# The 64 tokens left over by chunks of 1024: loads of their own, or a ninth token in half of the last chunk's partitions

## The chip, the cores and the metric

The kernel runs on one core of a Trainium2 chip. The metric is the time of one execution on the device, in microseconds (us), as the median of three runs. The profile is that of one further execution; its times count from its first instruction.

## What is computed

Four batches of 6208 tokens with 256 channels go through an attention over channels and then a mixture of depths, in which only 128 tokens of each batch pass a small network:

```python
qn = q / (np.linalg.norm(q, axis=1, keepdims=True) + 1e-06)      # norms over the tokens
kn = k / (np.linalg.norm(k, axis=1, keepdims=True) + 1e-06)
s = kn.transpose(0, 2, 1) @ qn / tau                             # 256 x 256 for each batch
a = softmax(s)                                                   # over the last axis
x = v @ a                                                        # tokens x 256
scores = x @ w_gate
top_idx = np.argpartition(-scores[b], 128)[:128]                 # the 128 best of each batch
ye = np.maximum(x[b, top_idx] @ w1, 0.0) @ w2
out = x;  out[b, top_idx] += sigmoid(scores[b, top_idx])[:, None] * ye
```

q, k, v and the output are fp32 in HBM, 25.4 MB each. The kernel computes in bf16 with fp32 sums.

## The kernel before, in words

**Tiles.** The tokens of a batch are cut into 6 full chunks of 1024 (`CHUNK`, `NFULL` = 6) and 64 tokens that are left over (`REM`). A full chunk is a tile of 128 partitions with 8 tokens in each (`RPP` = 8): partition p holds tokens 8p to 8p + 7 of the chunk, which lie one behind the other in HBM, so that a load is one run of 8 KB for each partition. The leftover tokens are a seventh chunk (`ci == NFULL`) with a tile of its own (`q_rem`, `k_rem`, `v_rem`, `stage_rem` from `rem_pool`), one token in each of 64 partitions.

**Loads.** `emit_load` issues them from GpSimd's queue[...]: 512 KB as written for a full chunk, 32 KB for a leftover. `units` lists them in the order of use, and `pump` issues the next one while buffers are free (4 for q and k, 6 for v, 2 for the leftovers of each kind) and no more than 11 tiles are ahead (`AHEAD`). When the last step that reads a chunk has been written, `consumed` gives its buffer back. The very last chunk of q and k (`halved`) is loaded in two halves of its tokens. Each load also waits until the load eight issues earlier has landed, as eight semaphores go round.

**First pass** (`p1_steps`): for each token row of a chunk, six matmuls add k'q, q'q and k'k to two PSUM tiles (L303, L305, L307). After a batch's last row, which is the leftover's, the softmax follows in stages (`softmax_stages`), put between the matmuls of the next batch.

**Second pass**: `p2_transpose` turns four token rows of v by TensorE and copies them from PSUM (`vt_sb`, L414 to L420), `p2_score` gives the gate's score for each token (L439), `p2_out` the output rows (L485), which ScalarE copies into a store tile (`stage`, L493). A store of a chunk is 1 MB from SyncE's queue (`emit_store`, L559). Batches 0 and 1 do this while the next batch is in its first pass; batch 2 does part of it, and batch 3 all of it, in the tail.

**Selection** (`select_stages`): a search over thresholds on VectorE finds the 128 best tokens, and a one-hot matmul gathers for each its place: `mps` holds for each chosen token a column's number of tokens before it and its partition. The token's row number `idx` is put together from the column (`toff`, by the weights `wrow`), the partition times 8, or the partition alone where the token is a leftover one (`fl`, L653 to L656). By this number the rows of v are gathered (L660), pass the network (`mlp_stages`), and are scattered over the stored output (L729), once the stores of that batch have landed.

**What stands late.** Batch 1 (`H`) keeps its chunks 4 and 5 in SBUF; its chosen tokens are added there by a one-hot matmul (`late_onehot`, `late_mm`), and these two chunks are stored last of all, chunk 5 in two halves. Chunk 3 of batch 1 and the first chunks of batch 2 are held back until the last loads are nearly through (`flush_deferred`): the stores are made to wait for the fourth and third last entry of `units`, chunks 3 and 4 of v of batch 3. In the tail SyncE's queue thus holds, in this order: chunk 3 of batch 1 in quarters, six chunks of batch 2, two leftovers, six chunks of batch 3, chunk 4 of batch 1, chunk 5 of batch 1 in halves.

All instructions stand in the order in which the program writes them (`plan`); no scheduler moves them.

Of the kernel before, what the change touches and what calls it, by code (L numbers as in the profile page):

```python
# [9 lines left out]
F32 = mybir.dt.float32  # L10
BF16 = mybir.dt.bfloat16
# [3 lines left out]
ALU = mybir.AluOpType  # L15
AX = mybir.AxisListType

P = 128
RPP = 8
CHUNK = RPP * P  # L20
# [6 lines left out]
def kernel(  # L27
# [28 lines left out]
    QK_BUFS = 4  # L56
    V_BUFS = 6
    ST_BUFS = 8
    VT_BUFS = 22
    EARLY = 4  # L60
    HOLD = 3
    AHEAD = 11
# [23 lines left out]
    v_flat = v.rearrange("b n c -> (b n) c")  # L86
    out_flat = out.rearrange("b n c -> (b n) c")

    def view(t, b, ci):
        if ci < NFULL:  # L90
            return t[b, ci * CHUNK:(ci + 1) * CHUNK, :].rearrange("(p s) c -> p s c", s=RPP)
        return t[b, NFULL * CHUNK:N, :]

# [54 lines left out]
    plan += [("tail",)] + T[:2] + rest[:1] + T[2:4] + [("adv",), ("a", L)] + T[4:6] + rest[1:2]  # L148
    plan += T[6:8] + W + T[8:10] + S[:6] + T[10:] + rest[2:3] + [("side",)] + S[6:]
    rest = rest[3:]  # L150
    units = []
    for op in plan:
        if op[0] in ("p1", "T"):
            u = ("qk", op[1], op[2]) if op[0] == "p1" else ("v", op[1], op[2][0])
            if u not in units:
                units.append(u)
    loaded = {}
    load_inst = {}
    state = {"next": 0, "qk": 0, "v": 0, "qkr": 0, "vr": 0}
    ahead = [0]  # L160
    limit = {"qk": QK_BUFS, "v": V_BUFS, "qkr": 2, "vr": 2}

    def bucket(kind, ci):
        return kind if ci < NFULL else kind + "r"

    halved = ("qk", B - 1, NFULL - 1)

    def emit_load(u):
        kind, b, ci = u
        tiles = []  # L170
        for nm, src in ((("q", q), ("k", k)) if kind == "qk" else (("v", v),)):
            if ci < NFULL:
                pool = qk_pool if kind == "qk" else v_pool
                t = pool.tile([P, RPP, C], BF16, name=f"{nm}_ch")
                if u != halved:
                    ins = nc.gpsimd.dma_start(out=t, in_=view(src, b, ci))  # L176
            else:
                t = rem_pool.tile([P, 1, C], BF16, name=f"{nm}_rem")
                ins = nc.gpsimd.dma_start(out=t[:REM, 0, :], in_=view(src, b, ci))
            tiles.append(t)  # L180
        if u == halved:
            h = RPP // 2
            for half in (slice(0, h), slice(h, RPP)):
                for t, src in zip(tiles, (q, k)):
                    ins = nc.gpsimd.dma_start(out=t[:, half, :], in_=view(src, b, ci)[:, half, :])
        loaded[u] = tiles
        load_inst[u] = ins

    def pump(most=1000):
        while state["next"] < len(units) and most > 0:  # L190
            u = units[state["next"]]
            bk = bucket(u[0], u[2])
            if state[bk] >= limit[bk] or ahead[0] >= AHEAD:
                return
            emit_load(u)
            ahead[0] += 2 if u[0] == "qk" else 1
            state[bk] += 1
            state["next"] += 1
            most -= 1

    def consumed(u):
        state[bucket(u[0], u[2])] -= 1
        ahead[0] -= 2 if u[0] == "qk" else 1
        pump()

# [51 lines left out]

    wrow = const.tile([P, B, NCOL + 1], F32)
    nc.vector.memset(wrow, 1.0)
    nc.vector.memset(wrow[:, :, RPP - 1:NCOL - 1:RPP], float(CHUNK - RPP + 1))  # L260
    nc.vector.memset(wrow[:, :, NCOL - 1:NCOL], 0.0)
    for b in range(B):
        nc.vector.memset(wrow[:, b, NCOL:NCOL + 1], float(b * N))
# [3 lines left out]
    for i in range(NSTEP):  # L267
# [11 lines left out]
    nc.vector.tensor_copy(rhs[:, NCOL + 2:NCOL + 3], iota_col)  # L279
    ones_col = const.tile([P, NCOL], BF16)  # L280
    nc.vector.memset(ones_col, 1.0)

# [5 lines left out]
    def p1_steps(b, ci):  # L288

        if b not in acc:  # L290
            acc[b] = (ps_s.tile([P, 2, C], F32, name="s_ps"), ps_g.tile([P, 4, P], F32, name="g_ps"))
        s_ps, g_ps = acc[b]
        qt, kt = loaded[("qk", b, ci)]
        rows = RPP if ci < NFULL else 1
        parts = P if ci < NFULL else REM

        def step(s):
            first = ci == 0 and s == 0
            last = ci == NFULL
            qs, ks = qt[:parts, s, :], kt[:parts, s, :]  # L300
            for cc in range(2):
                sl = slice(cc * P, (cc + 1) * P)
                nc.tensor.matmul(s_ps[:, cc, :], lhsT=ks[:, sl], rhs=qs,  # L303
                                 start=first and cc == 0, stop=last and cc == 1)
                nc.tensor.matmul(g_ps[:, cc, :], lhsT=qs[:, sl], rhs=qs[:, sl],  # L305
                                 start=first and cc == 0, stop=False)
# [100 lines left out]
    def p2_transpose(b, g, on_act=False):  # L407
        ci, s0, n = g
        parts = P if ci < NFULL else REM
        vt = loaded[("v", b, ci)][0]  # L410
        vt_ps = vt_psum()
        for j in range(n):
            for cc in range(2):
                nc.tensor.transpose(vt_ps[:, cc, j, :parts], in_=vt[:parts, s0 + j, cc * P:(cc + 1) * P],  # L414
                                    identity=ident_b[:parts, :parts])
# [115 lines left out]

    def late_onehot(idx):

        base = float(H * N + LATE[0] * CHUNK)
        at = moe.tile([P, 1], F32, name="late_at")
        nc.vector.tensor_copy(at, idx)
        nc.vector.tensor_scalar(out=at, in0=at, scalar1=-base, scalar2=1.0 / RPP, op0=ALU.add, op1=ALU.mult)
        onehot = moe.tile([P, len(LATE), RPP, P], BF16, name="late_onehot")
        for i in range(len(LATE)):
            at_row = moe.tile([P, RPP], F32, name=f"late_at_row{i}")  # L540
            nc.vector.tensor_scalar(out=at_row, in0=iota_row[:, 0:RPP], scalar1=-1.0 / RPP, scalar2=at,
                                    op0=ALU.mult, op1=ALU.add)
            nc.vector.tensor_tensor(out=onehot[:, i, :, :], in0=iota_row[:, None, :].to_broadcast([P, RPP, P]),
                                    in1=at_row[:, :, None].to_broadcast([P, RPP, P]), op=ALU.is_equal)
            if i + 1 < len(LATE):
                nc.vector.tensor_scalar(out=at, in0=at, scalar1=-float(P), scalar2=None, op0=ALU.add)
        late_moe.append(onehot)

    def emit_store(b, ci, rows=(0, RPP), count=1):
        st = stage_of[(b, ci)]  # L550
        pieces = []
        if ci == NFULL:
            pieces.append((view(out, b, ci), st[:REM, 0, :]))
        else:
            n = (rows[1] - rows[0]) // count
            for r in range(rows[0], rows[1], n):
                pieces.append((view(out, b, ci)[:, r:r + n, :], st[:, r:r + n, :]))
        for dst, src in pieces:
# [11 lines left out]
    def select_stages(b):  # L570
# [55 lines left out]
        with nc.allow_low_precision(reason="counts of at most 49 are whole in bf16"):  # L626
# [26 lines left out]
        nc.vector.scalar_tensor_tensor(out=fl, in0=toff, scalar=float(b * N + NFULL * CHUNK) - 0.5,  # L653
                                       in1=mps[:, NCOL + 1:NCOL + 2], op0=ALU.is_lt, op1=ALU.mult)
        idx = moe.tile([P, 1], I32, name="idx", bufs=3)
        nc.vector.tensor_scalar(out=idx, in0=mps[:, NCOL + 2:NCOL + 3], scalar1=fl, scalar2=toff,  # L656
                                op0=ALU.max, op1=ALU.add)
# [121 lines left out]
    def flush_deferred():  # L779
# [1 line left out]

        first = len(stores)
        emit_store(*deferred.pop(0), count=4)
        for piece, u in ((first, units[-4]), (first + 2, units[-3])):
            tc.add_manual_dep(
                stores[piece][1].ins, load_inst[u].ins.name,
                mybir.DependencyInfo(mybir.DependencyClass.Sync, mybir.DependencyReason.DATA),
# [6 lines left out]
    def do_p1(b, ci, s):  # L794
        if s == 0:
            pump()
            using(("qk", b, ci))
        steps = p1_steps(b, ci)
        steps[s]()
        spent(0.43)  # L800
        if s == len(steps) - 1:
            consumed(("qk", b, ci))

    def do_transpose(b, g, on_act=False):
        using(("v", b, g[0]))
        vts[(b, g)] = p2_transpose(b, g, on_act)
        if g[1] == 4 or g[0] == NFULL:
            consumed(("v", b, g[0]))
        spent(0.11 * g[2])

    def do_score(b, g):
# [129 lines left out]
```

## Time and profile before

| | |
|---|---|
| time, median of 3 runs | 261.95 us (261.92 to 263.41) |
| span in the profile | 260.1 us |
| TensorE busy with matmuls | 201.7 us, 78% |
| VectorE, ScalarE, GpSimd busy | 49%, 32%, 21% |
| moved by DMA | 66.84 MB, mean 257 GB/s |
| loads with a cast (GpSimd's queue) | 12384 packets, 38.93 MB |
| stores (SyncE's queue) | 4768 packets, 27.53 MB |
| loads of a full chunk of v | 24, 14.8 us from issue to landing in the median |
| loads of a leftover of v | 4, 16.8 us |
| stores of a full chunk | 22, 8.0 us |

The megabytes of a load with a cast are those that it writes, bf16; it reads twice as many. The time from issue to landing of one transfer is mostly its wait in the queue behind others. In the stretches that the prediction shows, DMA's share is the mean busy share of the core's 16 DMA engines; a little over 1 means that the records of neighbouring packets overlap.

### The profile page before, as it was taken

The numbers are of one execution on the slowest core, as the hardware profiler recorded it, in microseconds if no ns is written. First come the engines' busy times: TensorE is split into PE (matmuls) and PEld (weight loads), VectorE is DVE, ScalarE is ACT, GpSimd is POOL, SyncE is SP. The second block draws the span as 40 slices with busy tenths as digits, with TensorE's granted clock in tenths as the row PEclk, the third lists the DMA queues.
The fourth block names the chain that finished last, engine by engine and source line by source line (L and its number), as shares of the span: only waits on it lengthen the run. The fifth ranks groups of instructions, "written<-read, shape, count | busy, mean of one in ns | idle before, by whom it ended". The sixth has DMA issues, their size and how long they took to land.

```text
span 260.1 us, 6113 instructions
## 1 busy us (share of the span) xinstructions
PE 201.7 (78%) x2586; PEld 177.3 (68%) x2586; DVE 126.9 (49%) x474; ACT 84.3 (32%) x149; POOL 55.6 (21%) x104
## 2 busy tenths in 40 slices
PE   0199668889938688698997888799999878889920
PEld 0088557789927476598996677698999668568710
DVE  0300003624403366622436888666685865887830
ACT  3700000167720000107770100434110964878010
POOL 7104124121110023222300325230334003001110
PEclk9999999999976589689999999999999999999995
DMA  7999999999999999999999999999999999999980
GB/s 240 262 213 212 212 212 214 215 214 281 317 317 317 304 213 213 214 212 210 292 316 273 214 212 223 212 213 214 212 210 212 217 257 419 402 412 391 415 369 1
DMA packets 17181, 66.84 MB, mean 257 GB/s; under 512 B 2050, under 2 KB 3587, under 8 KB 14211
## 3 DMA queue, kind: packets, MB, share of 16 engines
q0 software_dynamic: 12384, 38.93, 75.0%
q1 hardware_dynamic: 4768, 27.53, 26.2%
q8 instruction: 20, 0.33, 0.4%
q14 instruction: 7, 0.05, 0.0%
q10 hardware_dynamic: 2, 0.00, 0.0%
HBM read 78.91 MB, written 25.95 MB: 403 GB/s over the span
## 4 chain that ended last, share of the span: by engine, by line
DMA 57%; PE 16%; issue 15%; DVE 6%; POOL 2%; POOLq 1%; ACT 0%
DMA k_ch<-in_k_dram 22%; DMA q_ch<-in_q_dram 18%; DMA v_ch<-in_v_dram 12%; PE s_ps L303 4%; PE o_ps L485 4%; DMA out_dram<-upd,idx 3%; DMA out_dram<-stage 2%; PE g_ps L307 2%; PE g_ps L305 2%; PE vt_ps L414 2%; DVE cnt L610 1%; DVE cmp L606 1%; PE sc_ps L439 1%; DVE junk L322 1%; PE m_ps L354 1%
## 5 line engine op out<-in xcount | busy, mean ns | idle before, releaser
L303 PE MATMUL s_ps<-q_ch,k_ch 128*128 128x256 bf16 x384 | 95.4, 289 | 20.9 <-DMA k_ch<-in_k_dram 20.3
L305 PE MATMUL g_ps<-q_ch 128*128 128x128 bf16 x384 | 88.1, 229 | 1.1 <-DVE nsq L322 1.0
L307 PE MATMUL g_ps<-k_ch 128*128 128x128 bf16 x384 | 88.1, 229 | 0.0
L303 PEld LDWEIGHTS <-k_ch 128*128 128x128 bf16 x384 | 39.7, 103 | 26.8 <-DMA k_ch<-in_k_dram 23.9
L485 PE MATMUL o_ps<-a_sb,vt_sb 128*128 128x256 bf16 (+1 forms) x322 | 47.1, 271 | 2.0 <-ACT vt_sb L418 1.3
L493 ACT COPY stage<-o_ps 128x512 f32<-128x512 f32 x75 | 42.2, 590 | 15.9 <-PE o_ps L485 15.8
L307 PEld LDWEIGHTS <-k_ch 128*128 128x128 bf16 x384 | 39.7, 103 | 8.2 <-issue 1.6
L305 PEld LDWEIGHTS <-q_ch 128*128 128x128 bf16 x384 | 39.6, 103 | 1.2 <-issue 0.9
L420 DVE COPY vt_sb<-vt_ps 128x1024 bf16<-128x1024 bf16 (+1 forms) x35 | 22.2, 637 | 31.5 <-PE vt_ps L414 31.5
L485 PEld LDWEIGHTS <-vt_sb 128*128 128x128 bf16 (+1 forms) x392 | 30.5, 97 | 8.3 <-issue 4.5
L318 ACT COPY s_sb<-s_ps 128x512 f32<-128x512 f32 x4 | 2.3, 585 | 85.3 <-PE s_ps L303 55.1
L439 PEld LDWEIGHTS <-vt_sb 128*128 128x128 bf16 x392 | 25.3, 96 | 2.7 <-DVE sc L574 0.2
L414 PEld LDWEIGHTS <-v_ch 128*128 128x128 bf16 x384 | 22.2, 97 | 5.6 <-DMA v_ch<-in_v_dram 4.4
L439 PE MATMUL sc_ps<-aw_sb,vt_sb 128*128 128x2 bf16 x392 | 25.7, 164 | 0.0
L176 POOL DMA_DIRECT2D q_ch<-in_q_dram x23 | 12.7, 553 | 60.3 <-PE g_ps L307 40.6
L414 PE MATMUL vt_ps<-ident_b,v_ch 128*128 128x128 bf16 x336 | 24.6, 219 | 1.2 <-ACT vt_sb L418 0.7
L322 DVE CUSTOM_DVE_ANT_0 junk<-g_ps,ident_f 128x128 bf16<-128x128 f32 x16 | 4.6, 290 | 34.8 <-PE g_ps L307 34.4
L176 POOL DMA_DIRECT2D v_ch<-in_v_dram x24 | 12.8, 539 | 23.8 <-DMA q_ch<-in_q_dram 11.0
L176 POOL DMA_DIRECT2D k_ch<-in_k_dram x23 | 12.5, 544 | 22.8 <-PE o_ps L485 10.6
L418 ACT COPY vt_sb<-vt_ps 128x1024 bf16<-128x1024 bf16 x11 | 10.6, 1012 | 14.1 <-PE vt_ps L414 14.0
L610 DVE TENSOR_REDUCE cnt<-cmp 128x7 bf16<-128x343 bf16 x28 | 14.4, 513 | 1.0
L606 DVE SCALAR_TENSOR_TENSOR cmp<-u,delta,shares 128x343 bf16<-128x343 f32 x24 | 13.9, 579 | 0.9
(161 smaller groups left out, 214.5 us busy)
## 6 DMA issues: line engine op xcount, KB each, us to landing
out_dram<-stage SPq DMA_DIRECT2D x22, 1024.0 KB, 8.0
v_ch<-in_v_dram POOLq DMA_DIRECT2D x24, 512.0 KB, 14.8
q_ch<-in_q_dram POOLq DMA_DIRECT2D x23, 512.0 KB, 16.8
k_ch<-in_k_dram POOLq DMA_DIRECT2D x23, 512.0 KB, 16.9
stage<-in_moe_w_dram SPq DMA_DIRECT2D x2, 1024.0 KB, 7.0
out_dram<-stage SPq DMA_DIRECT2D x4, 256.0 KB, 5.6
out_dram<-stage SPq DMA_DIRECT2D x2, 512.0 KB, 6.2
q_ch<-in_q_dram POOLq DMA_DIRECT2D x2, 256.0 KB, 9.0
```

What stands on the lines that cost most here:

```text
L176: ins = nc.gpsimd.dma_start(out=t, in_=view(src, b, ci))
L303: nc.tensor.matmul(s_ps[:, cc, :], lhsT=ks[:, sl], rhs=qs, start=first and cc == 0, stop=last and cc == 1)
L305: nc.tensor.matmul(g_ps[:, cc, :], lhsT=qs[:, sl], rhs=qs[:, sl], start=first and cc == 0, stop=False)
L307: nc.tensor.matmul(g_ps[:, 2 + cc, :], lhsT=ks[:, sl], rhs=ks[:, sl], start=False, stop=last and cc == 1)
L414: nc.tensor.transpose(vt_ps[:, cc, j, :parts], in_=vt[:parts, s0 + j, cc * P:(cc + 1) * P], identity=ident_b[:parts, :parts])
L418: nc.scalar.copy(vt_sb[:, :, :n, :parts], vt_ps[:, :, :n, :parts])
L420: nc.vector.tensor_copy(vt_sb[:, :, :n, :parts], vt_ps[:, :, :n, :parts])
L439: nc.tensor.matmul(sc_ps[:parts, col, :], lhsT=vt_sb[:, cc, j, :parts], rhs=aw_sb[:, cc, :], start=cc == 0 and col in (0, NCOL - 1), stop= ...
L485: nc.tensor.matmul(o_ps[:parts, pj, :], lhsT=vt_sb[:, cc, j, :parts], rhs=a_sb[:, cc, :], start=pj == 0 and cc == 0, stop=pj == m - 1 and ...
L493: nc.scalar.copy(st[:parts, s0 + pair * 2:s0 + pair * 2 + m, :], o_ps[:parts, :m, :])
L606: nc.vector.scalar_tensor_tensor(out=cmp, in0=wide, scalar=delta, in1=thr, op0=ALU.subtract, op1=ALU.is_ge)
L610: nc.vector.tensor_reduce(out=cnt, in_=cmp, axis=AX.X, op=ALU.add)
```

## The change

The leftover tokens get no tile and no load of their own. The last full chunk and the 64 tokens behind it are taken as one chunk of 1088 tokens: partitions 0 to 63 hold nine tokens each, partitions 64 to 127 eight. All chunk tiles of q, k and v get room for a ninth row. Since the two halves of the partitions have runs of different length, the chunk is loaded in two transfers (`pieces`), one for partitions 0 to 63 and one for 64 to 127; the halved last chunk of q and k in four transfers each of 64 partitions in place of two of 128. Twelve small loads go, and twelve chunk loads become two each.

The computation keeps its seventh step: the ninth row is read where the leftover tile was read, with 64 partitions. The output's ninth row keeps its tile `stage_rem` and its store of 64 KB, now to 64 rows of HBM that lie nine apart. The store of a last chunk is in two transfers as well; that of batch 1's last chunk, which was in two halves, in four. For the larger tiles the transposed v gets 20 buffers in place of 22. The partition's first token is now 9p for p up to 64, and 8p + 64 beyond; `wrow`, `rhs`, the last steps to `idx` and `late_onehot` follow that.

```diff
-    VT_BUFS = 22
+    VT_BUFS = 20
...
+    def pieces(t, b, ci, rows):
+        if ci < NFULL - 1:
+            v = t[b, ci * CHUNK:(ci + 1) * CHUNK, :].rearrange("(p s) c -> p s c", s=RPP)
+            return [(v[:, rows[0]:rows[1], :], slice(0, P), slice(*rows))]
+        mid = (NFULL - 1) * CHUNK + REM * (RPP + 1)
+        lo = t[b, (NFULL - 1) * CHUNK:mid, :].rearrange("(p s) c -> p s c", s=RPP + 1)
+        got = [(lo[:, rows[0]:rows[1], :], slice(0, REM), slice(*rows))]
+        if rows[0] < RPP:
+            hi = t[b, mid:N, :].rearrange("(p s) c -> p s c", s=RPP)
+            rows = (rows[0], min(rows[1], RPP))
+            got.append((hi[:, rows[0]:rows[1], :], slice(REM, P), slice(*rows)))
+        return got
...
-    limit = {"qk": QK_BUFS, "v": V_BUFS, "qkr": 2, "vr": 2}
+    limit = {"qk": QK_BUFS, "v": V_BUFS}
...
-            if ci < NFULL:
-                pool = qk_pool if kind == "qk" else v_pool
-                t = pool.tile([P, RPP, C], BF16, name=f"{nm}_ch")
-                if u != halved:
-                    ins = nc.gpsimd.dma_start(out=t, in_=view(src, b, ci))
-            else:
-                t = rem_pool.tile([P, 1, C], BF16, name=f"{nm}_rem")
-                ins = nc.gpsimd.dma_start(out=t[:REM, 0, :], in_=view(src, b, ci))
...
+        tiles = [pool.tile([P, RPP + 1, C], BF16, name=f"{nm}_ch") for nm, _ in srcs]
+        top = RPP + (ci == NFULL - 1)
+        for rows in [(0, RPP // 2), (RPP // 2, top)] if u == halved else [(0, top)]:
+            for t, (_, src) in zip(tiles, srcs):
+                for dram, parts, rr in pieces(src, b, ci, rows):
+                    ins = nc.gpsimd.dma_start(out=t[parts, rr, :], in_=dram)
...
-            qs, ks = qt[:parts, s, :], kt[:parts, s, :]
+            row = s if ci < NFULL else RPP
+            qs, ks = qt[:parts, row, :], kt[:parts, row, :]
...
         if ci == NFULL:
-            pieces.append((view(out, b, ci), st[:REM, 0, :]))
+            dram, parts, _ = pieces(out, b, NFULL - 1, (RPP, RPP + 1))[0]
+            todo.append((dram, st[parts, :, :]))
         else:
             n = (rows[1] - rows[0]) // count
             for r in range(rows[0], rows[1], n):
-                pieces.append((view(out, b, ci)[:, r:r + n, :], st[:, r:r + n, :]))
+                for dram, parts, rr in pieces(out, b, ci, (r, r + n)):
+                    todo.append((dram, st[parts, rr, :]))
...
-        for piece, u in ((first, units[-4]), (first + 2, units[-3])):
+        for piece, u in ((first, units[-3]), (first + 2, units[-2])):
...
-        if s == len(steps) - 1:
-            consumed(("qk", b, ci))
+        if s == len(steps) - 1 and ci != NFULL - 1:
+            consumed(("qk", b, home(ci)))
```

In `late_onehot` three small VectorE instructions are added, which work out the first token of each partition; the last two instructions before the gather (`fl`, `idx`) keep their number.

More of the change, by code (lines that the diff above doesn't have):

```diff
@@ L87 @@
     out_flat = out.rearrange("b n c -> (b n) c")
-    def view(t, b, ci):
-        if ci < NFULL:
-            return t[b, ci * CHUNK:(ci + 1) * CHUNK, :].rearrange("(p s) c -> p s c", s=RPP)
-        return t[b, NFULL * CHUNK:N, :]
+    def pieces(t, b, ci, rows):
[10 more added lines that the diff above has]
+        return got
     def groups(ci):
@@ L150, with home @@
     rest = rest[3:]
+    def home(ci):
+        return min(ci, NFULL - 1)
     units = []
@@ L153 @@
         if op[0] in ("p1", "T"):
-            u = ("qk", op[1], op[2]) if op[0] == "p1" else ("v", op[1], op[2][0])
+            u = ("qk", op[1], home(op[2])) if op[0] == "p1" else ("v", op[1], home(op[2][0]))
             if u not in units:
@@ L158 @@
     load_inst = {}
-    state = {"next": 0, "qk": 0, "v": 0, "qkr": 0, "vr": 0}
+    state = {"next": 0, "qk": 0, "v": 0}
     ahead = [0]
-    limit = {"qk": QK_BUFS, "v": V_BUFS, "qkr": 2, "vr": 2}
-    def bucket(kind, ci):
-        return kind if ci < NFULL else kind + "r"
+    limit = {"qk": QK_BUFS, "v": V_BUFS}
     halved = ("qk", B - 1, NFULL - 1)
@@ L169, in emit_load @@
         kind, b, ci = u
-        tiles = []
-        for nm, src in ((("q", q), ("k", k)) if kind == "qk" else (("v", v),)):
-            if ci < NFULL:
-                pool = qk_pool if kind == "qk" else v_pool
-                t = pool.tile([P, RPP, C], BF16, name=f"{nm}_ch")
-                if u != halved:
-                    ins = nc.gpsimd.dma_start(out=t, in_=view(src, b, ci))
-            else:
-                t = rem_pool.tile([P, 1, C], BF16, name=f"{nm}_rem")
-                ins = nc.gpsimd.dma_start(out=t[:REM, 0, :], in_=view(src, b, ci))
[L180 to L185, printed above, removed]
+        srcs = (("q", q), ("k", k)) if kind == "qk" else (("v", v),)
+        pool = qk_pool if kind == "qk" else v_pool
+        tiles = [pool.tile([P, RPP + 1, C], BF16, name=f"{nm}_ch") for nm, _ in srcs]
[4 more added lines that the diff above has]
+                    ins = nc.gpsimd.dma_start(out=t[parts, rr, :], in_=dram)
         loaded[u] = tiles
@@ L191, in pump @@
             u = units[state["next"]]
-            bk = bucket(u[0], u[2])
+            bk = u[0]
             if state[bk] >= limit[bk] or ahead[0] >= AHEAD:
@@ L201, in consumed @@
     def consumed(u):
-        state[bucket(u[0], u[2])] -= 1
+        state[u[0]] -= 1
         ahead[0] -= 2 if u[0] == "qk" else 1
@@ L259 @@
     nc.vector.memset(wrow, 1.0)
-    nc.vector.memset(wrow[:, :, RPP - 1:NCOL - 1:RPP], float(CHUNK - RPP + 1))
+    nc.vector.memset(wrow[:, :, RPP - 1:NCOL - 2:RPP], float(CHUNK - RPP + 1))
     nc.vector.memset(wrow[:, :, NCOL - 1:NCOL], 0.0)
@@ L278 @@
                             scalar2=None, op0=ALU.mult)
-    nc.vector.tensor_copy(rhs[:, NCOL + 2:NCOL + 3], iota_col)
+    nc.vector.tensor_scalar(out=rhs[:, NCOL + 2:NCOL + 3], in0=iota_col, scalar1=float(REM),
+                            scalar2=None, op0=ALU.min)
     ones_col = const.tile([P, NCOL], BF16)
@@ L292, in p1_steps @@
         s_ps, g_ps = acc[b]
-        qt, kt = loaded[("qk", b, ci)]
+        qt, kt = loaded[("qk", b, home(ci))]
         rows = RPP if ci < NFULL else 1
@@ L409, in p2_transpose @@
         parts = P if ci < NFULL else REM
-        vt = loaded[("v", b, ci)][0]
+        vt = loaded[("v", b, home(ci))][0]
+        row = s0 if ci < NFULL else RPP
         vt_ps = vt_psum()
@@ L413, in p2_transpose @@
             for cc in range(2):
-                nc.tensor.transpose(vt_ps[:, cc, j, :parts], in_=vt[:parts, s0 + j, cc * P:(cc + 1) * P],
+                nc.tensor.transpose(vt_ps[:, cc, j, :parts], in_=vt[:parts, row + j, cc * P:(cc + 1) * P],
                                     identity=ident_b[:parts, :parts])
@@ L532, in late_onehot @@
     def late_onehot(idx):
-        base = float(H * N + LATE[0] * CHUNK)
         at = moe.tile([P, 1], F32, name="late_at")
         nc.vector.tensor_copy(at, idx)
-        nc.vector.tensor_scalar(out=at, in0=at, scalar1=-base, scalar2=1.0 / RPP, op0=ALU.add, op1=ALU.mult)
+        first = moe.tile([P, D], F32, name="gy")[:, 0:P]
         onehot = moe.tile([P, len(LATE), RPP, P], BF16, name="late_onehot")
-        for i in range(len(LATE)):
+        for i, ci in enumerate(LATE):
+            if ci < NFULL - 1:
+                nc.vector.tensor_scalar(out=first, in0=iota_row, scalar1=float(RPP), scalar2=None, op0=ALU.mult)
+            else:
+                nc.vector.tensor_scalar(out=first, in0=iota_row, scalar1=float(REM), scalar2=None, op0=ALU.min)
+                nc.vector.scalar_tensor_tensor(out=first, in0=iota_row, scalar=float(RPP), in1=first,
+                                               op0=ALU.mult, op1=ALU.add)
             at_row = moe.tile([P, RPP], F32, name=f"late_at_row{i}")
-            nc.vector.tensor_scalar(out=at_row, in0=iota_row[:, 0:RPP], scalar1=-1.0 / RPP, scalar2=at,
-                                    op0=ALU.mult, op1=ALU.add)
-            nc.vector.tensor_tensor(out=onehot[:, i, :, :], in0=iota_row[:, None, :].to_broadcast([P, RPP, P]),
+            nc.vector.tensor_scalar(out=at_row, in0=iota_row[:, 0:RPP], scalar1=float(H * N + ci * CHUNK),
+                                    scalar2=None, op0=ALU.add)
+            nc.vector.tensor_scalar(out=at_row, in0=at_row, scalar1=-1.0, scalar2=at, op0=ALU.mult, op1=ALU.add)
+            nc.vector.tensor_tensor(out=onehot[:, i, :, :], in0=first[:, None, :].to_broadcast([P, RPP, P]),
                                     in1=at_row[:, :, None].to_broadcast([P, RPP, P]), op=ALU.is_equal)
-            if i + 1 < len(LATE):
-                nc.vector.tensor_scalar(out=at, in0=at, scalar1=-float(P), scalar2=None, op0=ALU.add)
         late_moe.append(onehot)
@@ L550, in emit_store @@
         st = stage_of[(b, ci)]
-        pieces = []
+        todo = []
         if ci == NFULL:
-            pieces.append((view(out, b, ci), st[:REM, 0, :]))
+            dram, parts, _ = pieces(out, b, NFULL - 1, (RPP, RPP + 1))[0]
+            todo.append((dram, st[parts, :, :]))
         else:
@@ L556, in emit_store @@
             for r in range(rows[0], rows[1], n):
-                pieces.append((view(out, b, ci)[:, r:r + n, :], st[:, r:r + n, :]))
-        for dst, src in pieces:
+                for dram, parts, rr in pieces(out, b, ci, (r, r + n)):
+                    todo.append((dram, st[parts, rr, :]))
+        for dst, src in todo:
             ins = nc.sync.dma_start(out=dst, in_=src)
@@ L652, in select_stages @@
         fl = moe.tile([P, 1], F32, name="fl")
-        nc.vector.scalar_tensor_tensor(out=fl, in0=toff, scalar=float(b * N + NFULL * CHUNK) - 0.5,
-                                       in1=mps[:, NCOL + 1:NCOL + 2], op0=ALU.is_lt, op1=ALU.mult)
+        nc.vector.scalar_tensor_tensor(out=fl, in0=toff, scalar=float(b * N + (NFULL - 1) * CHUNK) - 0.5,
+                                       in1=mps[:, NCOL + 2:NCOL + 3], op0=ALU.is_ge, op1=ALU.mult)
         idx = moe.tile([P, 1], I32, name="idx", bufs=3)
-        nc.vector.tensor_scalar(out=idx, in0=mps[:, NCOL + 2:NCOL + 3], scalar1=fl, scalar2=toff,
-                                op0=ALU.max, op1=ALU.add)
+        nc.vector.tensor_scalar(out=idx, in0=mps[:, NCOL + 1:NCOL + 2], scalar1=fl, scalar2=toff,
+                                op0=ALU.add, op1=ALU.add)
         yield
@@ L796, in do_p1 @@
             pump()
-            using(("qk", b, ci))
+            using(("qk", b, home(ci)))
         steps = p1_steps(b, ci)
@@ L800, in do_p1 @@
         spent(0.43)
-        if s == len(steps) - 1:
-            consumed(("qk", b, ci))
+        if s == len(steps) - 1 and ci != NFULL - 1:
+            consumed(("qk", b, home(ci)))
     def do_transpose(b, g, on_act=False):
-        using(("v", b, g[0]))
+        using(("v", b, home(g[0])))
         vts[(b, g)] = p2_transpose(b, g, on_act)
-        if g[1] == 4 or g[0] == NFULL:
-            consumed(("v", b, g[0]))
+        if (g[1] == 4 and g[0] != NFULL - 1) or g[0] == NFULL:
+            consumed(("v", b, home(g[0])))
         spent(0.11 * g[2])
```

## The prediction

> **What bounds the kernel now.** I read the page's slices and its queue table first, then busy time by stage, then the chain of waits near the end, then single transfers with their time from issue to landing. The slices say whether a resource ever rests:
>
> ```profile
> PE   0199668889938688698997888799999878889920
> DMA  7999999999999999999999999999999999999980
> ...
> q0 software_dynamic: 12384, 38.93, 75.0%
> q1 hardware_dynamic: 4768, 27.53, 26.2%
> ...
> DMA 57%; PE 16%; issue 15%; DVE 6%; POOL 2%; POOLq 1%; ACT 0%
> ```
>
> TensorE has holes; the 16 DMA engines have none between the second slice and the 38th. The two queues (q0: loads that cast fp32 to bf16, issued by GpSimd; q1: stores, issued by SyncE) add up to 101% of 16 engines' span, and the chain is mostly DMA. So the time is the engine time of all transfers, some 4 us at the start and some 6 us after the last one. By stage (the columns are stretch, us, busy time of each engine, PEclk, DMA share, GB/s):
>
> ```profile
> 10.00:60.00 50.00, 38.96 (x491) 34.97 (x492) 8.34 (x36) 8.82 (x15) 11.70 (x22) 1.00 1.07 213
> 60.00:90.00 30.00, 22.09 (x269) 19.59 (x267) 9.34 (x25) 10.30 (x19) 3.70 (x7) 0.81 1.04 314
> 141.00:209.00 68.00, 59.04 (x829) 52.86 (x828) 51.79 (x194) 18.59 (x36) 18.11 (x32) 1.00 1.08 214
> 216.00:252.00 36.00, 29.72 (x321) 24.29 (x318) 26.21 (x90) 20.74 (x41) 4.93 (x5) 1.00 1.01 410
> 252.00:260.00 8.00, 0.00 (x0) 0.00 (x0) 0.00 (x0) 0.00 (x0) 0.00 (x0) 0.55 0.11 45
> ```
>
> Loads alone move 213 to 214 GB/s (counted at the bf16 side), loads beside stores 314, stores alone 410. From 216 to 252 us nothing but stores and a few gathers and scatters runs, with the engines full: engine time added there moves the end one for one. The chain agrees (start, us, what):
>
> ```profile
> 188.18 10.43 DMA k_ch<-in_k_dram
> 198.62 0.28 issue
> 198.90 16.20 DMA v_ch<-in_v_dram
> ...
> 230.03 5.89 DMA out_dram<-stage
> ...
> 243.05 6.80 DMA out_dram<-upd,idx
> ```
>
> Loads set it up to 215.1 us, stores and scatters afterwards. The last two transfers are level: the last store is issued at 248.9 and lands 5.2 us later (254.1), the last scatter at 250.6 and lands 3.8 later (254.4).
>
> [...] Does the trace agree? The only 64-partition stores in it are those of the leftover tokens:
>
> ```profile
> out_dram<-stage_rem SPq DMA_DIRECT2D x4, 64.0 KB, 6.2
> q_rem<-in_q_dram POOLq DMA_DIRECT2D x4, 32.0 KB, 19.9
> ```
>
> Two of them run back to back in the full tail. The 1 MB store ahead of them, issued at 225.7, lands after 7.4 us (233.1); the 1 MB store behind, issued at 230.0, after 5.9 (235.9). That is 2.8 us for 1 MB and 128 KB; stores of 1 MB alone land 2.45 us apart. So the 128 KB took about 0.35 us: 0.31 at 410 GB/s[...]. The windows say the same:
>
> ```profile
> 228.00:230.30 2.30, 1.72 (x16) 1.24 (x14) 2.09 (x8) 1.78 (x4) 0.00 (x0) 1.00 1.02 417
> 230.30:233.10 2.80, 2.22 (x21) 1.84 (x21) 2.28 (x11) 2.21 (x5) 0.00 (x0) 1.00 0.98 392
> 233.10:236.00 2.90, 2.82 (x30) 2.30 (x28) 1.70 (x9) 2.90 (x7) 0.08 (x1) 1.00 1.01 424
> ```
>
> The dip from 417 to 392 is small. But these are 8 KB an engine[...], and the engines aren't in step: the packets of the two stores, 46 ns each and 8 to an engine, are spread from 230.4 to 233.0 us. So the trace [...] doesn't show 64 partitions of half a megabyte.
>
> **The change part by part.**
>
> 1. Twelve leftover loads go (q, k and v of four batches, 32 KB each). Three landings price one: k issued at 188.2 lands after 10.4 (198.6), the q leftover issued at 188.7 after 10.1 (198.8), the k leftover at 189.2 after 9.8 (199.0): 0.2 us each. 12 x 0.2 = 2.4 us of load queue, all on the path.
>
> 2. The same bytes come back as a ninth token in 64 partitions: 32 KB at 214 GB/s is 0.15 us, 12 x 0.15 = 1.8 us. Net -0.6 us. If the longer rows (4608 bytes) are cut in two it is 0; if the ninth token rode for nothing, -2.4.
>
> 3. The last chunk's loads are two transfers of 64 partitions. [...] I take no cost. [...]
>
> 4. GpSimd issues 2 DMAs more (the halved last q and k become 8 issues where 4 and 2 leftovers stood). An issue takes 0.53 us and up to eight are in flight, 10 to 16 us ahead of their landing; the issues hide behind the queue. A load waits for the landing of the one eight issues back; with 128 KB pieces in the ring the last v loads are issued while at least seven pieces (0.6 us each, 4.3 us) are still to come, so the engines don't run dry.
>
> 5. The chunk's buffer is held for one more TensorE step, which the load of the next batch waits for: some 0.65 us on a load that lands 10 us or more after issue. No cost. The cap of 11 on loads ahead no longer counts leftovers, so real loads start earlier; with engines already full this gives nothing.
>
> 6. VectorE: three small instructions more in the one-hot of the late batch (0.15 to 0.3 us each, at 156 us, DVE busy 52 of 68 us in that stage), behind them only the gather's issue on GpSimd, with loads queued. The rebuilt token index costs nothing: the same two instructions. 20 in place of 22 transposed buffers: the transpose at the end of the last batch then needs the group of the batch before that TensorE has already multiplied earlier in its own order. No wait. TensorE's work is unchanged.
>
> 7. Stores of a last chunk are two transfers of 64 partitions. Batch 0's falls into a stage where stores get half of the engines' time (about 200 GB/s[...]): no cost taken[...]. Those of batches 2, 3 and 1 fall into the tail: 3.1 MB, at 410 GB/s 7.7 us[...]. [...] a half takes an engine 1.25 us, and engines are up to 2.5 us apart, most of them under 1 us. I take [...] +4.4 us.
>
> Sum: 261.95 - 0.6 + 4.4 = 265.8 us.
>
> **The rivals.**
>
> [...] the small stores passed at nearly full rate, and the engines are spread. Then only step 2 remains: 261.4 us, no change.
>
> Full serialization: [...] every half store in the tail pays[...]: 269.0 us. Against it: the spread of the engines.
>
> Faster by over 1%: steps 2 at its best (-2.4) and the last loads landing a little earlier, so that the selection of the last batch (218.7 to 235.6 us, a serial chain) starts earlier: some 259.0 us. Against it: the tail is full of stores, which an earlier start of that chain doesn't shorten, and the bytes loaded are the same.
>
> **How the numbers follow.** Partial collision (265.8) 0.40[...] (261.4) 0.37, full serialization (269.0) 0.13, faster (259.0) 0.10. The likeliest gives 265.8. The range 260.6 to 268.2 leaves out the faster case and the upper part of serialization. 1% is 2.6 us: slower (over 264.6) takes nearly all of the partial case and the full one, 0.51; faster 0.10; the rest, 0.39, is within 1%.
>
> **What would show it.** Right: in the tail the stores of 64 partitions land markedly later than half of 2.45 us after each other, the tail's GB/s falls from 410 towards 350 with the DMA share still at 1, the loads before 209 us end 0.5 us earlier or level, and the last stores, not the scatter, end the chain. Wrong: half stores landing 1.2 us apart at 410 GB/s[...], or load stages below 213 GB/s (step 3 is dear), or DMA slices under 9 before the tail (step 4 or 5 starves the queue).

## The result, and the profile after

The changed kernel takes 265.72 us (median of 4 runs, 265.30 to 267.13), against 261.94 for the kernel before on the same chip (4 runs, 261.69 to 263.41): 1.0135 times as long, 95% interval 1.0087 to 1.0183. The prediction was 265.8. Executions of one kernel lie up to 3.1 us apart and a profile can be of a longer one (that of the changed kernel is of its longest, 267.13 us, that of before of one of 262.14), in which the tail moves 391 to 397 GB/s even where no store is cut into lower and upper halves there, so packet durations are given beside rates.

The page of the changed kernel, the rows that answer to those shown of before (slices of 6.6 us, queues, chain):

```profile
PE   0198688899951977799995796899999698798600
DMA  7999999999999999999999999999999999999980
GB/s 237 258 217 213 215 213 211 216 209 285 314 319 315 299 214 214 212 215 223 337 310 216 212 215 212 221 216 212 212 199 214 216 382 399 347 371 393 292 297 9
...
q0 software_dynamic: 11648, 38.93, 73.3%
q1 hardware_dynamic: 4848, 27.53, 27.5%
...
DMA 35%; PE 30%; DVE 16%; issue 10%; ACT 2%; POOL 2%; POOLq 1%; SPq 0%; DVEq 0%
```

The DMA engines are as full as before, from the second slice to the 38th. What differs is how long the two queues keep them: the loads (q0) 73.3% of 265.3 us, 194.5 us, where before they took 75.0% of 260.1, 195.1; the stores (q1) 27.5% of 265.3, 73.0 us, where before 26.2% of 260.1, 68.1. The same 27.53 MB of SyncE's queue (all stores, and 2.1 MB of weights at the start) take each engine 4.8 us more. By stage (stretch, us, busy time of each engine, PEclk, DMA share, GB/s):

```profile
10.00:60.00 50.00, 39.56 (x485) 35.42 (x486) 7.88 (x37) 8.73 (x14) 11.71 (x22) 0.97 1.06 213
60.00:90.00 30.00, 21.43 (x285) 19.37 (x284) 10.94 (x29) 10.40 (x19) 3.69 (x7) 0.91 1.04 309
...
141.00:209.00 68.00, 59.46 (x833) 53.46 (x832) 51.30 (x193) 17.27 (x35) 18.99 (x34) 1.00 1.07 213
...
216.00:252.00 36.00, 29.91 (x323) 24.37 (x320) 26.49 (x90) 20.77 (x41) 3.97 (x4) 1.00 1.01 366
252.00:258.00 6.00, 0.00 (x0) 0.00 (x0) 0.00 (x0) 0.00 (x0) 0.97 (x1) 0.50 0.91 310
258.00:265.00 7.00, 0.00 (x0) 0.00 (x0) 0.00 (x0) 0.00 (x0) 0.00 (x0) 0.50 0.07 25
```

Up to 209 us little has moved: 213 GB/s where 213 and 214 stood, 309 where 314 stood. The tail has: from 216 to 252 us the engines are still full (share 1.01) but move 366 GB/s in place of 410, and from 252 to 258 they are still at 0.91, where before they had fallen to 0.15:

```profile
252.00:258.00 6.00, 0.00 (x0) 0.00 (x0) 0.00 (x0) 0.00 (x0) 0.00 (x0) 0.57 0.15 59
```

The share is that of before and the rate lower, as the stores' packets take longer: of those of 8 KB after 216 us, 166 of 1636 take over 450 ns, where before 11 of 1624 did.

One store shows it. The answers for issues between 242 and 244 us, first of the kernel before, then of the changed kernel (operation, KB each, us from issue to landing):

```profile
out_dram<-stage SPq DMA_DIRECT2D x1, 1024.0 KB, 6.8
out_dram<-upd,idx POOLq DMA_INDIRECT x1, 6.8
```

```profile
out_dram<-stage SPq DMA_DIRECT2D x2, 512.0 KB, 9.6
out_dram<-upd,idx POOLq DMA_INDIRECT x1, 9.1
```

This is the last chunk of batch 3: 1 MB before, two halves of it after, which land 9.6 us after issue in the median, the second 3.7 us after the first (250.3 and 253.9). And it does more than take longer. The waits of GpSimd from 236 to 262 us, before and then after (engine, line, waited for: us in total, times, longest):

```profile
...
POOL out_dram L729 <- DVE upd L723: 12.8, 2, 6.6
```

```profile
...
POOL out_dram L743 <- DMA out_dram<-stage: 11.0, 1, 11.0
POOL out_dram L743 <- DVE upd L737: 6.2, 1, 6.2
```

Before, the last scatter waited for VectorE's `upd` and was issued at 250.6 us. Now it waits for the store of its batch's last chunk, whose second half lands at 253.9, is issued at 255.1 and lands at 260.5. The chain of waits of the changed kernel ends in that store (start, us, what); the 9.89 us of `issue` are the scatter's wait for it:

```profile
242.25 0.47 SPq L573
242.77 1.35 DMA out_dram<-stage
244.12 9.89 issue
...
254.85 1.20 POOLq L950
```

### The profile page after: what moved, and what is told of

It reads as the page before. It is cut to its first block, busy times and chain, and to the rows that moved or that the text cites. A ratio compares the mean times of both kernels' runs of the same rounds, so it can differ in the third digit from the quotient of the medians.

```text
span 265.3 us, 6134 instructions
## 1 busy us (share of the span) xinstructions
PE 200.8 (76%) x2586; PEld 177.2 (67%) x2586; DVE 127.7 (48%) x477; ACT 84.3 (32%) x149; POOL 56.5 (21%) x106
## 3 DMA queue, kind: packets, MB, share of 16 engines
q0 software_dynamic: 11648, 38.93, 73.3%
q1 hardware_dynamic: 4848, 27.53, 27.5%
## 4 chain that ended last, share of the span: by engine, by line
DMA 35%; PE 30%; DVE 16%; issue 10%; ACT 2%; POOL 2%; POOLq 1%; SPq 0%; DVEq 0%
DMA k_ch<-in_k_dram 25%; PE o_ps L492 8%; PE s_ps L309 7%; DMA v_ch<-in_v_dram 6%; PE vt_ps L421 4%; DMA q_ch<-in_q_dram 4%; PE g_ps L313 3%; PE g_ps L311 3%; DVE cnt L624 3%; DVE cmp L620 3%; PE sc_ps L446 1%; ACT vt_sb L425 1%; DVE junk L328 1%; POOL v_ch L188 1%; PE m_ps L360 1%
## 5 line engine op out<-in xcount | busy, mean ns | idle before, releaser
L309 PE MATMUL s_ps<-q_ch,k_ch 128*128 128x256 bf16 x392 | 96.8, 287 | 21.3 <-DMA k_ch<-in_k_dram 18.6
L311 PE MATMUL g_ps<-q_ch 128*128 128x128 bf16 x392 | 89.5, 228 | 2.0 <-DVE nsq L328 2.0
L313 PE MATMUL g_ps<-k_ch 128*128 128x128 bf16 x392 | 89.6, 229 | 0.0
L309 PEld LDWEIGHTS <-k_ch 128*128 128x128 bf16 x392 | 40.4, 103 | 26.8 <-DMA k_ch<-in_k_dram 22.6
L313 PEld LDWEIGHTS <-k_ch 128*128 128x128 bf16 x392 | 40.4, 103 | 9.0 <-issue 2.5
L311 PEld LDWEIGHTS <-q_ch 128*128 128x128 bf16 x392 | 40.3, 103 | 1.7 <-issue 1.4
L188 POOL DMA_DIRECT2D q_ch<-in_q_dram x30 | 16.5, 550 | 71.4 <-PE g_ps L313 41.3
L421 PE MATMUL vt_ps<-ident_b,v_ch 128*128 128x128 bf16 (+1 forms) x344 | 25.5, 218 | 1.3 <-ACT vt_sb L425 0.7
L421 PEld LDWEIGHTS <-v_ch 128*128 128x128 bf16 x392 | 23.0, 97 | 3.9 <-issue 1.9
L188 POOL DMA_DIRECT2D k_ch<-in_k_dram x30 | 16.1, 540 | 43.8 <-DMA k_ch<-in_k_dram 14.1
L188 POOL DMA_DIRECT2D v_ch<-in_v_dram x28 | 14.9, 532 | 26.0 <-DMA q_ch<-in_q_dram 12.1
```

Source lines behind the costliest of these rows:

```text
L188: ins = nc.gpsimd.dma_start(out=t[parts, rr, :], in_=dram)
L309: nc.tensor.matmul(s_ps[:, cc, :], lhsT=ks[:, sl], rhs=qs, start=first and cc == 0, stop=last and cc == 1)
```

## The experiments

Times are medians in us, beside a median of the kernel before on the same chip (262.22 for the first four, 262.40 for the next four, then 262.37, and 262.27 for the last). The ratio with its 95% interval is worked out from all executions of both kernels; costs in us are taken from it (1% is 2.6 us), so they can differ from the difference of two medians. First the question whether the loss is in the stores or in the loads, and whether it is the number of transfers. Theory A in the forecasts below puts the loss down to the 64 partitions that a store in the tail takes, and from the run with even and odd partitions on to which 64 they are: the lower or the upper half is slow. That a half would be slow by itself was the author's estimate; no trace had shown it.

**The changed kernel with whole stores.**

```diff
-                for dram, parts, rr in pieces(out, b, ci, (r, r + n)):
-                    todo.append((dram, st[parts, rr, :]))
+                whole = out[b, ci * CHUNK:(ci + 1) * CHUNK, :].rearrange("(p s) c -> p s c", s=RPP)
+                todo.append((whole[:, r:r + n, :], st[:, r:r + n, :]))
```

> The changed kernel, with its loads, but the stores of the last chunks whole: 8 rows of all 128 partitions in one transfer (two for batch 1's), and the leftover's 64 rows behind them, placed in HBM as the kernel before places them. This changes what is written where (the tokens of the last chunk land in other rows), not how much. Theory A[...] (transfers of 64 partitions in the store-only tail are slow[...]): 261.4 us, the whole loss is gone. Theory B, number of transfers (every further store costs SyncE's issue and a completion): 261.4 too. Theory C, loads (the half loads or the ninth token cost the time): still about 265.7.

Measured: 262.67, ratio 1.0006 (0.9988 to 1.0023). The tail:

```profile
216.00:252.00 36.00, 29.43 (x317) 24.17 (x315) 25.93 (x90) 20.77 (x41) 4.93 (x5) 1.00 1.02 411
```

The loss is gone and the rate is back. (Here the last chunk's tokens land in wrong rows of the output, so this kernel serves for timing only.) All that the change does to loads, buffers and VectorE together costs nothing that can be measured; the loss is in the stores.

**The kernel before with its last chunks stored in partition halves**, and the same with the cut across the rows of tokens:

```diff
-                pieces.append((view(out, b, ci)[:, r:r + n, :], st[:, r:r + n, :]))
+                cuts = [slice(0, 64), slice(64, P)] if ci == NFULL - 1 else [slice(0, P)]
+                for cut in cuts:
+                    pieces.append((view(out, b, ci)[cut, r:r + n, :], st[cut, r:r + n, :]))
```

> The kernel before, with one edit: the stores of each batch's last chunk are cut into partitions 0 to 63 and 64 to 127. Loads as before. A[...]: 261.95 + 4.4 = 266.3 us, the tail's GB/s falls as in the changed kernel. B (number of transfers): also about 266. C (loads): 262.0.

> The kernel before, with the stores of each batch's last chunk cut into as many transfers as in the run with partition halves, but by token rows: each covers all 128 partitions with half of the bytes for each. A[...]: 262.0 us, no loss. B (number of transfers): about 266, as with partition halves. C (loads): 262.0.

Measured: partition halves 264.85, ratio 1.0088 (1.0063 to 1.0114); row halves 262.14, ratio 0.9999 (0.9978 to 1.0021). Their tails, in this order:

```profile
216.00:252.00 36.00, 30.01 (x327) 24.60 (x323) 26.41 (x90) 20.83 (x41) 3.96 (x4) 1.00 1.00 368
```

```profile
216.00:252.00 36.00, 29.86 (x324) 24.45 (x321) 26.35 (x90) 20.82 (x41) 4.93 (x5) 1.00 1.02 409
```

Twice as many transfers cost nothing when the cut is across the rows (with packets half as long, 5488 in SyncE's queue in place of 4768); cut by partitions (4848 packets), they cost 2.3 us in a kernel that is otherwise that of before.

**Is it 64 partitions, or which 64?** The same cut, but by even and odd partitions: same transfers, same bytes and packets.

```diff
-                cuts = [slice(0, 64), slice(64, P)] if ci == NFULL - 1 else [slice(0, P)]
+                cuts = [slice(0, P, 2), slice(1, P, 2)] if ci == NFULL - 1 else [slice(0, P)]
```

> The kernel before, with each store of a last chunk sent as two transfers of 64 partitions, the even ones and the odd ones, in place of the lower and the upper half. Same number of transfers, same 64 partitions and same bytes in each as with halves (264.85 us, 368 GB/s in the tail). Theory A[...] the time is that of before, 262.2 (261.6 to 262.9), and the tail moves some 410 GB/s. Rival B (a transfer of 64 partitions is slower by itself, whichever they are): 264.9 (264 to 266), some 368 GB/s.

Measured: 262.24, ratio 0.9990 (0.9973 to 1.0007). The engine time of its stores (SyncE's queue) is that of before, 68.3 us against 68.1. Then the same in the changed kernel, where `emit_store` sends the two halves from `st[0:P:2, ...]` and `st[1:P:2, ...]`, with the leftover row still from the lower 64 partitions, and again with tokens in wrong rows of the output, for timing only:

> The changed kernel, with the two stores of each last chunk reading the even and the odd partitions in place of the lower and the upper half; its rows then lie at other places of the output. Number, size and order of all transfers are as in the changed kernel (265.72 us). Theory A[...]: the loss goes, as with whole stores: 262.7 (262.0 to 263.4), with 410 GB/s in the tail. Rival B (number of transfers, or 64 partitions whichever they are): 265.7 (265 to 267), 366 GB/s.

Measured: 262.53, ratio 0.9995 (0.9972 to 1.0018). Its page and its tail:

```profile
GB/s 237 262 219 211 214 212 212 218 212 257 318 314 315 313 228 214 216 213 213 287 338 254 213 213 211 220 218 211 214 208 201 214 253 423 399 404 390 417 375 3
...
q0 software_dynamic: 11648, 38.93, 74.7%
q1 hardware_dynamic: 4848, 27.53, 26.1%
```

```profile
216.00:252.00 36.00, 30.30 (x332) 24.89 (x329) 26.41 (x90) 20.81 (x41) 4.93 (x5) 1.00 1.01 406
```

The packets in the queues are to the last one as many as in the changed kernel (11648 and 4848); what differs is which 64 partitions a half takes, and with it which rows of HBM it writes, and the loss is gone. A lower or upper half fills one half of the chunk's stretch of HBM, an even or odd one takes every second run of 8 KB in all of it. No run changes one without the other, so the runs rule out the number of partitions as the cause, but don't tell the side of SBUF from that of HBM. The issues between 242 and 244 us:

```profile
out_dram<-stage SPq DMA_DIRECT2D x2, 512.0 KB, 6.1
out_dram<-upd,idx POOLq DMA_INDIRECT x1, 6.4
```

These two land 1.2 us apart, not 3.7.

The packet records say how. Of the stores' packets of 8 KB after 216 us, the median is 309 ns in all kernels. Packets over 450 ns number 11 of 1624 before, 166 of 1636 in the changed kernel (mean 653 ns), 144 with partition halves in the kernel before, and 6 and 9 with even and odd partitions. Of the 166, 151 start from 228 to 234 and from 246 to 258 us, where the half stores pass. Only 256 of the 1636 belong to half stores (the last chunks of batches 2 and 3, 128 packets each), so most of theirs may be slow; a record doesn't tell its store. They don't share one slow rate: durations spread from the usual one to over 1 us, with a peak at 600 to 650 ns, about twice the median.

**More halved bytes, and halves elsewhere.** All stores of batch 3 in partition halves (`if b == B - 1` in the edit above), and batch 0's last chunk alone:

> The kernel before, with all stores of batch 3 (6.3 MB, all in the tail) sent in partition halves, and the last chunks of the other batches whole. With 3.1 MB in halves in the tail the loss was 2.6 us. Theory A[...]: 2.6 x 6.3 / 3.1 = 5.3 us more than before, 267.5 (265.8 to 269.0), and the excess spread over the whole stretch from 216 to 252 us. Rival C (only the very last stores count, which end the chain): as before with halves of the last chunks, 264.9 (264 to 265.6).

> The kernel before, with only batch 0's last chunk stored in partition halves, in the stage where loads take half of the engines. Theory A[...]: 262.2 (261.6 to 262.8). Rival F (each halved megabyte costs the same wherever it lies, 2.6 / 3.1 us per MB): 263.1 (262.7 to 263.7).

Measured: batch 3 266.84, ratio 1.0179 (1.0127 to 1.0231); batch 0 262.04, ratio 1.0002 (0.9984 to 1.0019). The rate of the batch 3 kernel falls where batch 3 is stored, in the 36th slice and after:

```profile
GB/s 239 261 214 213 213 213 213 214 214 298 317 317 313 284 210 214 212 215 223 315 319 228 211 218 217 211 215 214 211 209 214 218 370 399 404 305 329 349 342 5
...
q1 hardware_dynamic: 4864, 27.53, 27.2%
```

Twice the halved bytes (6.3 MB) cost 4.7 us (3.3 to 6.1) where 3.1 MB cost 2.3 (1.7 to 3.0), so rival C is out. How the cost grows with the bytes isn't settled. By the times it is about in proportion, but in the two profiles the engine time of the stores rises almost alike, to 72.0 us (27.2% of 264.7) and to 71.6 (27.2% of 263.4) from 68.1:

```profile
q1 hardware_dynamic: 4848, 27.53, 27.2%
```

Part of the time of the batch 3 kernel is again a wait: its last scatter is held for 11.0 us by its batch's last store. In the stage that loads and stores share (before, from 60 to 90 us, loads take 52.2% of the engines' time and stores 51.3%), 1 MB costs nothing that can be measured (at most 0.5 us), as theory A, which looks for the loss in the tail alone, had it.

**The loads.** The changed kernel loads 64 partitions at a time without loss (with whole stores its ratio was 1.0006). The same cut in the kernel before, which keeps its leftover loads, was to show that by itself:

```diff
+        cuts = [slice(0, 64), slice(64, P)] if ci == NFULL - 1 else [slice(0, P)]
...
-                    ins = nc.gpsimd.dma_start(out=t, in_=view(src, b, ci))
+                    for cut in cuts:
+                        ins = nc.gpsimd.dma_start(out=t[cut, :, :], in_=view(src, b, ci)[cut, :, :])
```

> The kernel before, with the loads of each batch's last chunk (q, k and v) cut into partitions 0 to 63 and 64 to 127; the leftovers keep their own loads, stores as before. A[...]: loads write at 214 GB/s[...]: 262.0 us, at most 0.5 more.[...] B (number of transfers): 262 to 263. C (loads): about 265.

Measured: 265.79, ratio 1.0110 (1.0082 to 1.0138), 2.9 us. That was a surprise, and three more runs asked whether it was which partitions a load takes (rival E), the number of issues (theory D), or the cut of the wide loads (rival G). The loads cut by token rows (`t[:, 0:4, :]` and `t[:, 4:8, :]`; the one that is halved already, in four), by even and odd partitions, and, with wide loads whole, the 12 leftover loads cut in two (`t[odd:REM:2, 0, :]`, `odd` 0 and 1):

> The kernel before, with the loads of the last chunks cut in two by token rows (128 partitions and half of the rows in each; the load that is cut by rows already, in four). As many issues as when they are cut into partition halves (265.8 us)[...]. Theory D (the partition-halved loads of the kernel before lost 3.6 us because 14 more issues fill the places in flight with small transfers, and GpSimd's gather and the last loads wait behind them): 265.8 (264.8 to 267). Rival E[...]: 262.2 (261.5 to 263).

> The kernel before, with the loads of the last chunks sent as two transfers of 64 partitions each, the even and the odd ones. Issues, packets and bytes are those of the lower and upper halves (265.79 us)[...]. Cutting by token rows (265.41 us) did not tell the causes apart, since it halved the packets and the engine time of the loads rose by 3.5 us of itself. Theory D (the loss of the halved loads in the kernel before is from 14 issues more: gather and last loads wait behind them): 265.8 (264.8 to 267). Rival E[...]: 262.2 (261.5 to 263).

> The kernel before, with each of the 12 leftover loads (64 partitions of 1 KB) sent as two, the even and the odd of its 64 partitions: 12 issues more on GpSimd and no byte, packet or wide transfer changed. Cutting the last chunks' loads in even and odd partitions (14 issues more) cost 3.6 us[...]. Theory D (the cost is one of issues, each of which takes a place in flight): 12/14 of it, 3.1 us, 265.4 (264.2 to 266.5). Rival G (the cost is one of cutting the wide loads, whose two pieces' packets follow each other worse): 262.4 (261.6 to 263.2).

Measured: token rows 265.41, ratio 1.0124 (1.0077 to 1.0171); even and odd 265.94, ratio 1.0140 (1.0094 to 1.0187); leftovers in two 264.59, ratio 1.0066 (1.0045 to 1.0087). The first tells nothing: a cut across the rows halves the packets, which makes the load queue itself longer (14400 packets and 75.6% of 262.6 us, 198.5, against 195.1).

```profile
q0 software_dynamic: 14400, 38.94, 75.6%
```

Even and odd partitions lose no less than lower and upper halves (3.7 us against 2.9, intervals that overlap), so for the loads it isn't which partitions (rival E falls). Twelve tiny issues more cost 1.7 us (1.2 to 2.3), between theory D's 3.1 and rival G's nothing: issues cost by themselves, though less than D said. Where some of it goes can be seen in the stretch from 196 to 200 us, for the kernel before, partition halves, even and odd, leftovers in two, and the changed kernel:

```profile
196.00:200.00 4.00, 4.00 (x60) 3.79 (x58) 2.36 (x12) 0.00 (x0) 2.10 (x4) 1.00 1.13 214
```

```profile
196.00:200.00 4.00, 4.00 (x60) 3.79 (x58) 2.99 (x11) 0.00 (x0) 3.49 (x7) 1.00 1.05 178
```

```profile
196.00:200.00 4.00, 4.00 (x61) 3.79 (x59) 2.26 (x12) 0.00 (x0) 3.45 (x7) 1.00 1.03 178
```

```profile
196.00:200.00 4.00, 4.00 (x60) 3.81 (x58) 2.37 (x12) 0.00 (x0) 2.09 (x4) 1.00 1.11 193
```

```profile
196.00:200.00 4.00, 4.00 (x59) 3.79 (x57) 3.22 (x13) 0.17 (x1) 2.50 (x5) 1.00 1.11 202
```

Here the loads in flight are the small pieces of the last q and k: 178 GB/s in place of 214 over 4 us is 0.7 us. In the packet records of both cuts of the last chunks' loads the packets in flight at once fall to 11 between 195 and 198 us, where before there are never fewer than 16, and a few packets of 4 KB (8 and 6 from 194 to 204 us) take over 450 ns, where before none does. That the queue holds too few bytes there is the likely reading, not shown. The load queue's engine time explains about as much again (74.8% of 261.9 us, 195.9, for even and odd, 0.8 more than before). Together that is most of the 1.8 us by which the profiled execution of even and odd, the shortest of its four, is longer than that of before; the rest of the 3.7 us was not isolated. In the kernel with partition halves the last v load lands at 217.1 us in place of 215.8, and the last gather but one is issued at 221.6 in place of 218.7.

**A part of the change alone.** q and k take the leftover tokens, v and all stores stay as before (`pieces` and `home` used for q and k only):

> A part of the change alone: q and k of the last chunk take the leftover tokens (nine in 64 partitions, two loads of 64 partitions, no leftover loads of q and k); v, the order of tokens on partitions in the output and all stores are as before. Theory A with issue counts ([...] two issues more than before): eight leftover loads less at 0.2 us, eight ninth tokens at 0.15, so 0.4 us less than before, 261.8 (261.0 to 262.6). Rival E ([...] 3.6 us for 18 of them): two thirds of it, 264.2 (263.5 to 265).

Measured: 262.49, ratio 1.0003 (0.9986 to 1.0019). No loss, and no gain that can be measured.

## Why the prediction was right, point by point

- Steps 1 and 2 (fewer leftover loads, -0.6 us): the engine time is there, 195.1 to 194.5 us, and the trace has 640 whole packets of 4608 bytes (361 ns, against 324 for 4096), so the longer rows are not cut. (The three landings that priced a leftover lie 0.18 us apart, not quite 0.2, so the sum should have come to -0.4.) In the time it doesn't show: with whole stores the ratio was 1.0006, with even and odd stores 0.9995, and with q and k alone 1.0003. Step 4 takes part of it back; the rest is below what these runs resolve.
- Step 3 (no cost of the half loads, an estimate of the author) held: the changed kernel with whole stores keeps the half loads and is level with before (1.0006). Lower and upper halves did lose 2.9 us in the kernel before, but even and odd ones lost as much there, so for another reason.
- Step 4 (issues hide) was right for the sum and wrong in its argument. That "the engines don't run dry" is not quite so: from 196 to 200 us the changed kernel moves 202 GB/s in place of 214, 0.2 us. With only two issues more it stays small; with 12 or 14 more it cost 1.7 to 3.7 us, which the argument would have put at nothing.
- Steps 5 and 6 (one step longer in the buffer, VectorE, 20 buffers): no cost. The changed kernel with whole stores holds all of them and is level with before.
- Step 7, mechanism: half stores in the tail cost time, and the even and odd pair shows that this depends on which half (ratio 1.0135 with lower and upper, 0.9995 with even and odd), not on 64 partitions as such. That lower and upper halves would collide, and only partly, was the author's estimate. Why they are slow, and whether it is their place in SBUF or the rows of HBM that they write, no run shows. Batch 0's halves cost nothing, as forecast (1.0002).
- Step 7, size: +4.4 us taken, an estimate of the author that rested on no trace; 3.7 measured (the ratios 1.0135 with halves and 0.9995 with even and odd differ by 1.4% of 262 us; the intervals leave 0.5% on the first and 0.2% on the second). The engine time of the stores rose by 4.8 us, near the estimate, but not all of it moves the end. In the kernel before the same cut cost 2.3 (3.5 us of engine time), so the cost isn't a constant; why it is less there stays open.
- The sum: the stores came out 0.7 us under the forecast and the loads 0.6 over it. That the total lies within 0.1 us is partly these two errors against each other.
- The signs: the tail fell from 410 to 366 GB/s with share 1.01, as named. The half stores land 3.7 us after each other, and the last chunk of v lands at 215.1 us as before. "The last stores, not the scatter, end the chain" was half of it: stores and scatter end level (260.2 and 260.5 us), because the scatter now waits for its batch's last store. The prediction had not named that wait.
- The rivals: no cost in the stores (261.4) and faster (259.0) are out by the tail, at 366 GB/s; full serialization (269.0, like the 4.4 an estimate that rested on no trace) is out by the time, whose longest execution is 267.13.

## What to carry to other kernels

When a tile of 128 partitions must be stored in two parts and the DMA engines are full with stores, cut it by even and odd partitions or by rows, not into lower and upper half: here that is 3.7 us or none (by rows, 2.3 or none in the kernel before). For this change the ninth token would have to lie on every second partition; no run has that with all tokens in their place. Ask of every split where it falls, since the same halves cost nothing that can be measured (at most 0.5 us for 1 MB) where stores share the engines with loads. And when queues are full, count issues as well as bytes: twelve small ones more cost 1.7 us here.

## What the runs showed that was not expected

- Two stores of 64 partitions each run at the full rate when they are interleaved (even and odd): 406 GB/s in the tail against 366. Theory A had forecast it, with no trace to rest on; so for the full rate of these stores one transfer over all 128 partitions isn't needed.
- The slowed packets of the tail take twice the usual time in the mean (653 ns against a median of 309), but spread from 450 ns to over 1 us, and not all packets of half stores are slow (166 over 450 ns, of 256).
- Cutting 12 loads of 32 KB in two, with no byte or packet of data changed, cost 0.66% (0.45 to 0.87), about 0.14 us for each issue more, though GpSimd was busy for only 23% of the span.
